# All five queues in written order, weight transfers gated on landed inputs, and four input buffers in a fused linear-attention and mixture kernel

## The chip, the cores and the metric

The kernel runs on one core of a Trainium2 chip. The metric is device time in microseconds (us) of one execution; lower is better. A profile of one execution shows the engines PE (TensorE matmuls), PEld (TensorE weight loads), DVE (VectorE), ACT (ScalarE), POOL (GpSimd) and SP (SyncE, which here only issues transfers).

## The reference

Two layers follow each other. The first is a linear attention with a decaying state; for each batch `b` (4) and head `h` (8), over 768 steps of width 48:

```python
for t in range(S):
    cur = np.einsum('bhd,bhe->bhde', u[None] * kt, vt)
    y[:, :, t] = np.einsum('bhd,bhde->bhe', rt, state + cur)
    state = w[None, :, :, None] * state + np.einsum('bhd,bhe->bhde', kt, vt)
```

Its output, as 3072 rows of 384, is `x` of the second layer, in which each of 4 experts is weighted per row:

```python
p = domain_probs / (domain_probs.sum(-1, keepdims=True) + 1e-09)
for e in range(E):
    h = np.maximum(x @ w1[e], 0.0)          # 384 -> 1024
    out += p[:, e:e + 1] * (h @ w2[e])      # 1024 -> 384
```

## The kernel before

Time is cut into 24 chunks of 128 rows: chunk `ci` is batch `ci % 4` and stretch `ci // 4`. A **super-chunk** `sc` is the four chunks of one stretch, so there are 6. All inputs come as float32; the weights are cast to bfloat16 by their transfer.

**A chunk's attention** goes through these steps, in this order. `pre` (L164) scales r and k by powers of w into the bfloat16 tile RK (L167, L168, DVE), forms `ruk` = r·k·u (L173, L174, POOL), casts v to Vb (L176, POOL), sums ruk into dcoef (L175, DVE) and makes dv (L177, POOL). `stRK` transposes RK on PE (L185, 8 matmuls) and ACT copies the result out (L189). `stAt` multiplies (L196) and DVE applies the mask (L202). `stY` forms the chunk's output on PE (L213, L220); DVE adds dv into Ysb (L224). `stS` updates the state: PE L235, then DVE L244 in the first super-chunk, later DVE L246 and POOL L247. `stX` transposes Ysb (L253) and DVE copies it to xTe (L254), the input of the experts. RK's transpose and stX share one PSUM buffer (tag "tr"); Y, St and the small constants share another (tag "ys").

**The experts.** `l1(e, sc, fb, ...)` is 3 matmuls (L266) and a Relu on ACT (L270); eight values of `fb` make one expert's hidden layer. `l2(e, sc, s)` is 8 matmuls of 384 columns for one chunk (L279), scaled and accumulated on DVE (L285, L287). One pair (e, sc) for a whole super-chunk is a **slot**: 8 l1 of 512 columns, in groups of two, and after each group one l2 of the slot before. Expert 0 of the first super-chunk is not a slot: it is done chunk by chunk (`fill`, L322), l1 with 128 columns. There follow 23 slots; numbered from 0, slots 0 to 2 are experts 1 to 3 of super-chunk 0, slot 3 is expert 0 of super-chunk 1. A counter `carry` inserts attention steps of later chunks between the groups: 10/12 of a step per group in slots 0 and 1, then 5/12 (L365).

**What sets the order.** PE's and POOL's queues are in written order (L318). DVE, ACT and SP are not: a scheduler puts their instructions in an order of its own. `pre` runs up to two chunks ahead of stRK (LEAD, L350). SP issues the loads of r, k and v (L80, three per chunk, six buffers each) and the stores (L290). POOL issues the eight weight transfers: w1 of expert 0 as its first instruction (L85), w2 of expert 0 after `pre(0)`, and the rest after `pre` of chunks 2 to 7 (table `after`, L296). `late_consts` (L132) prepares the decay wC and the normalised expert weights p_nat: p is normalised as 24 x 512, then transposed by PE (L151).

## Time and profile before

| what | value |
|---|---|
| three runs | 348.68, 345.33, 348.07 us; median 348.07 us |
| the profiled execution | 350.93 us, of which the span from first to last instruction is 348.9 us |
| busy in the span | PE 299.3 us (86%), DVE 171.0, ACT 143.3, POOL 108.0 us |
| transfers | 25.96 MB; loads and stores of SP 19.32 MB, weights of POOL 6.29 MB |
| mean granted TensorE clock | 0.964 of full speed |

Busy time counts an engine's instructions; the ends of matmuls are modelled, so busy time of PE is not the same as PE at full speed. "Granted clock" is the share of 2.4 GHz that the chip allowed TensorE in a stretch; the two levels are 1.2 and 2.4 GHz, so 0.76 is a mixture of both. The profiled execution is one of its own; it took 0.8% longer than the median of the three runs.

### The profile page before, as it was taken

The page shows a single profiled execution, that of the slowest core. Times are in us where ns is not written, and L with a number is a line of the kernel's source. Part 1 is how long each engine was busy: PE and PEld are TensorE (multiplying, and loading weights), DVE is VectorE, ACT ScalarE, POOL GpSimd, SP SyncE. Part 2 cuts the span into 40 slices and gives each one's busy share as a digit, 9 for nine tenths or more (in the row PEclk, how much of TensorE's full clock was granted, in tenths as well). Part 3 has the DMA queues.
Part 4 walks back from the last instruction along what each step waited for, and adds up shares of the span by engine and source line. Part 5 has one row for each costly group of instructions (what it writes and reads, how often), then busy time and mean ns, then how long its engine had stood idle before and what let it go on. Part 6 is the DMA issues. An engine that isn't in the chain of part 4 may idle for free.

```text
span 348.9 us, 5568 instructions
## 1 busy us (share of the span) xinstructions
PE 299.3 (86%) x2193; PEld 172.7 (50%) x2229; DVE 171.0 (49%) x333; ACT 143.3 (41%) x245; POOL 108.0 (31%) x145
## 2 busy tenths in 40 slices
PE   0026477767799999999999999999899999999995
PEld 0025455434455555555555555555455555555553
DVE  3498475555655556465546545553534243222223
...
GB/s 131 209 177 189 182 198 207 175 185 143 70 68 49 111 70 69 21 48 121 91 17 68 2 0 92 1 4 0 2 45 47 0 2 0 27 65 0 2 0 90
DMA packets 84457, 25.96 MB, mean 74 GB/s; under 512 B 75448, under 2 KB 82872, under 8 KB 84432
## 3 DMA queue, kind: packets, MB, share of 16 engines
q1 hardware_dynamic: 78672, 19.32, 25.8%
q0 software_dynamic: 5760, 6.29, 11.0%
...
q14 instruction: 8, 0.07, 0.1%
...
## 4 chain that ended last, share of the span: by engine, by line
PE 74%; POOL 11%; DVE 6%; issue 5%; SPq 3%; DMA 1%; POOLq 0%; DVEq 0%
PE out_ps L279 34%; PE hT_ps L266 32%; PE RKT_ps L185 3%; POOL ruk L174 3%; POOL ruk L173 3%; SPq L80 2%; PE At_ps L196 2%; POOL dv L177 1%; POOL S L247 1%; PE Y_ps L220 1%; DVE AtM L202 1%; PE Y_ps L213 1%; POOL Vb L176 1%; PE St_ps L235 1%; SPq L88 1%
## 5 line engine op out<-in xcount | busy, mean ns | idle before, releaser
L270 ACT ACTIVATE hTs<-hT_ps 128x512 bf16<-128x512 f32 (+1 forms) x216 | 116.6, 551 | 146.8 <-PE hT_ps L266 144.0
L266 PE MATMUL hT_ps<-xTe,w_sb 128*128 128x512 bf16 (+1 forms) x612 | 145.6, 366 | 3.3 <-DVE xTe L254 1.4
L279 PE MATMUL out_ps<-w_sb,hTs 128*128 128x384 bf16 x768 | 141.1, 328 | 0.0
L279 PEld LDWEIGHTS <-hTs 128*128 128x128 bf16 x768 | 73.5, 98 | 50.9 <-issue 1.0
L266 PEld LDWEIGHTS <-w_sb 128*128 128x128 bf16 x648 | 59.1, 103 | 50.6 <-issue 3.5
L287 DVE SCALAR_TENSOR_TENSOR oacc<-out_ps,p_nat,oacc 128x384 f32<-128x384 f32 x72 | 44.4, 616 | 73.0 <-PE out_ps L279 72.7
L247 POOL TENSOR_TENSOR S<-Tn,wC 64x192 bf16<-64x192 f32 x32 | 19.4, 605 | 111.5 <-DVE Tn L246 110.3
L189 ACT COPY RKT<-RKT_ps 128x1024 bf16<-128x1024 bf16 x24 | 24.3, 1012 | 45.6 <-PE RKT_ps L185 45.6
L185 PE MATMUL RKT_ps<-ident,RK 128*128 128x128 bf16 x192 | 16.8, 237 | 28.5 <-DVE xTe L254 14.3
L175 DVE TENSOR_REDUCE dcoef<-ruk 128x8 f32<-128x384 f32 x24 | 13.2, 551 | 48.9 <-POOL ruk L174 48.9
L185 PEld LDWEIGHTS <-RK 128*128 128x128 bf16 x192 | 14.2, 106 | 35.5 <-issue 18.3
L202 DVE TENSOR_TENSOR AtM<-At_ps,mask 128x512 bf16<-128x512 f32 x48 | 30.7, 681 | 0.1
L173 POOL TENSOR_TENSOR ruk<-Rt,Kt 128x384 f32<-128x384 f32 x24 | 24.4, 1015 | 9.4 <-DMA Kt<-in_k_dram 8.0
L285 DVE TENSOR_SCALAR oacc<-out_ps,p_nat 128x384 f32<-128x384 f32 x24 | 14.8, 616 | 23.5 <-PE out_ps L279 23.4
L174 POOL TENSOR_TENSOR ruk<-ruk,U_sd 128x384 f32<-128x384 f32 x24 | 24.9, 1039 | 2.2 <-DMA U_sd<-in_u_dram 0.4
L177 POOL TENSOR_TENSOR dv<-Vt,dcoef 128x384 f32<-128x384 f32 x24 | 20.2, 840 | 16.4 <-DVE dcoef L175 13.9
L167 DVE TENSOR_TENSOR RK<-Rt,W_sd 128x384 bf16<-128x384 f32 x24 | 16.1, 673 | 14.5 <-DMA Rt<-in_r_dram 6.1
L224 DVE TENSOR_TENSOR Ysb<-Y_ps,dv 128x384 bf16<-128x384 f32 x24 | 13.4, 557 | 11.0 <-PE Y_ps L220 11.0
L168 DVE TENSOR_TENSOR RK<-Kt,W_sd 128x384 bf16<-128x384 f32 x24 | 15.4, 643 | 0.6
L220 PE MATMUL Y_ps<-Vb,AtM 128*128 128x48 bf16 x192 | 9.8, 188 | 5.7 <-DVE AtM L202 5.7
L176 POOL CAST Vb<-Vt 128x384 bf16<-128x384 f32 x24 | 12.8, 532 | 0.0
L246 DVE TENSOR_TENSOR Tn<-S,St_ps 64x192 f32<-64x192 bf16 x32 | 11.1, 347 | 1.5 <-PE St_ps L235 1.0
...
## 6 DMA issues: line engine op xcount, KB each, us to landing
...
Rt<-in_r_dram SPq DMA_DIRECT2D x24, 192.0 KB, 4.4
Kt<-in_k_dram SPq DMA_DIRECT2D x24, 192.0 KB, 3.6
Vt<-in_v_dram SPq DMA_DIRECT2D x24, 192.0 KB, 3.7
out_dram<-oacc SPq DMA_DIRECT2D x24, 192.0 KB, 1.8
logw_bc<-in_w_dram SPq DMA_DIRECT2D x1, 192.0 KB
U_sd<-in_u_dram SPq DMA_DIRECT2D x1, 192.0 KB, 7.7
...
```

What stands on the lines that cost most here:

```text
L173: nc.gpsimd.tensor_mul(ruk, Rt, Kt)
L174: nc.gpsimd.tensor_mul(ruk, ruk, U_sd)
L176: nc.gpsimd.tensor_copy(Vb, Vt)
L177: nc.gpsimd.tensor_mul(dv, Vt, dcoef.to_broadcast((128, H, D)))
L185: nc.tensor.transpose(ps[:, i, q, :], s["RK"][:, i, 2 * q:2 * q + 2, :].rearrange("p a b -> p (a b)"), ident)
L189: nc.scalar.copy(s["RKT"], ps)
L202: nc.vector.tensor_mul(s["AtM"][:, j], ps[:, j], mask[:, None, :].to_broadcast((128, NP, C)))
L247: nc.gpsimd.tensor_mul(S_new[pr, :, cl], Tn[pr], wCb)
L266: nc.tensor.matmul(ps[:, 0:n, :].rearrange("p a b -> p (a b)"), w1_sb[:, e, db, fb * 128:(fb + 1) * 128], xTe[:, db, s0:s0 + n, :].rearran ...
L270: nc.scalar.activation(hTs[:, fb, s0:s0 + n, :], ps[:, 0:n, :], AF.Relu)
L279: nc.tensor.matmul(ps, hTs[:, fb, s, :], w2_sb[:, e, fb, :], start=(fb == 0), stop=(fb == NFB - 1))
L287: nc.vector.scalar_tensor_tensor(oaccs[ci], in0=ps, scalar=pe, in1=oaccs[ci], op0=ALU.mult, op1=ALU.add)
```

## The change

- All five queues, DVE, ACT and SP among them, are put in written order.
- `pre` is split. `pre_a` has the RK products, ruk and Vb; `pre_b` has the reduction, dv and the issue of one later chunk's load. Neither runs ahead by LEAD any longer; each chunk has six steps instead of five, and its steps are not interleaved with those of the chunk before, but for chunks 2 and 3.
- Input buffers go from six to four. The loads of chunks 0 to 2 are issued first, each later one in `pre_b` of the chunk three before it.
- Each weight transfer is preceded on POOL by a copy of one element of that chunk's r into the weight tile (table `gated`), so that it can't start before this r has landed. w1 of expert 0 waits for r of chunk 0, w2 of expert 0 for chunk 1, expert 1 for chunk 3, expert 2 for chunk 4, expert 3 for chunk 6.
- The raw p is transposed, and normalised after that as 128 x 24 (`p_consts`), behind the first chunk's attention. The state tiles are cleared at the start.
- Two l1 of slot 0 are done ahead, before the last chunk of super-chunk 0 is finished. Slots 0 to 2 take 0.72 of a step per group, and later ones 0.5.

```diff
-    NIN = 6
+    NIN = 4
     NRK = 4
-    LEAD = 2
...
-    logw_bc = consts.tile([128, HD], F32)
-    nc.sync.dma_start(logw_bc, w.rearrange("h d -> (h d)")[None, :].to_broadcast((128, HD)))
-    load_w1(0)
+    w_bc = consts.tile([128, HD], F32)
+    nc.sync.dma_start(w_bc, w.rearrange("h d -> (h d)")[None, :].to_broadcast((128, HD)))
     load(0)
+
+    wrow = consts.tile([NP, 2, P2], F32)
+    nc.vector.memset(wrow, 1.0)
+    nc.sync.dma_start(wrow[:, :, 0:D], w.rearrange("(q j) d -> q j d", j=2))
     U_sd = consts.tile([128, H, D], F32)
     nc.sync.dma_start(U_sd.rearrange("p h d -> p (h d)"),
                       u.rearrange("h d -> (h d)")[None, :].to_broadcast((128, HD)))
-    load(1)
-
-    wrow = consts.tile([NP, 2, P2], F32)
-    nc.vector.memset(wrow, 1.0)
-    nc.sync.dma_start(wrow[:, :, 0:D], w.rearrange("(q j) d -> q j d", j=2))
     prow = consts.tile([TOTC, C, E], F32)
     nc.sync.dma_start(prow, moe_domain_probs.rearrange("(n p) e -> n p e", p=C))
+    load(1)
+    load(2)
...
+    RKB = [consts.tile([128, 2, H, P2], BF16, name=f"RK{i}") for i in range(NRK)]
+    for t in RKB:
+        nc.vector.memset(t[:, :, :, D:P2], 0.0)
+
+    Sbd = [[consts.tile([128, NP, 2 * D], BF16, name=f"S{b}_{i}") for i in range(2)]
+           for b in range(B)]
+    for b in range(B):
+        for i in range(2):
+            nc.vector.memset(Sbd[b][i], 0.0)
...
-    def late_consts():
-        for b in range(B):
-            for i in range(2):
-                nc.vector.memset(Sbd[b][i], 0.0)
+    def w_consts():
         ps = psum.tile([128, NP], F32, tag="ys", bufs=1, name="w_ps")
         nc.tensor.transpose(ps, wrow.rearrange("q j d -> q (j d)"), ident_f[0:NP, 0:NP])
         nc.vector.tensor_copy(wC, ps)
         for _ in range(7):
             nc.vector.tensor_mul(wC, wC, wC)
-        p_sum = consts.tile([TOTC, C, 1], F32)
-        nc.vector.reduce_sum(p_sum, prow, axis=AX.X)
-        nc.vector.tensor_scalar(p_sum, p_sum, scalar1=1e-9, scalar2=None, op0=ALU.add)
-        p_rec = consts.tile([TOTC, C, 1], F32)
-        nc.vector.reciprocal(p_rec, p_sum)
-        p_e = consts.tile([TOTC, E, C], F32)
-        nc.vector.tensor_mul(p_e, prow.rearrange("n p e -> n e p"),
-                             p_rec.rearrange("n p o -> n o p").to_broadcast((TOTC, E, C)))
+
+    def p_consts():
         pp = psum.tile([128, E, TOTC], F32, tag="ys", bufs=1, name="p_ps")
         for e in range(E):
-            nc.tensor.transpose(pp[:, e, :], p_e[:, e, :], ident_f[0:TOTC, 0:TOTC])
-        nc.vector.tensor_copy(p_nat, pp)
+            nc.tensor.transpose(pp[:, e, :], prow[:, :, e], ident_f[0:TOTC, 0:TOTC])
+        p_sum = consts.tile([128, TOTC, 1], F32)
+        nc.vector.reduce_sum(p_sum, pp.rearrange("p e n -> p n e"), axis=AX.X)
+        nc.vector.tensor_scalar(p_sum, p_sum, scalar1=1e-9, scalar2=None, op0=ALU.add)
+        p_rec = consts.tile([128, TOTC, 1], F32)
+        nc.vector.reciprocal(p_rec, p_sum)
+        nc.vector.tensor_mul(p_nat, pp,
+                             p_rec.rearrange("p n o -> p o n").to_broadcast((128, E, TOTC)))
...
-
-    def pre(ci):
+    loaded = [3]
+
+    def pre_a(ci):
         Rt, Kt, Vt = ins.pop(ci)
+        if ci in gated:
+
+            for load_w, t in gated[ci]:
+                nc.gpsimd.tensor_copy(t, Rt[0:1, 0, 0:1])
+                load_w()
         RK = RKB[ci % NRK]
         nc.vector.tensor_mul(RK[:, 0, :, 0:D], Rt, W1_sd)
         nc.vector.tensor_mul(RK[:, 1, :, 0:D], Kt, W2_sd)
         ruk = work.tile([128, H, D], F32, tag="ruk", name="ruk")
-        dcoef = work.tile([128, H, 1], F32, tag="dcoef", name="dcoef")
         Vb = work.tile([128, H, D], BF16, tag="Vb", name="Vb")
-        dv = work.tile([128, H, D], F32, tag="dv", name="dv")
         nc.gpsimd.tensor_mul(ruk, Rt, Kt)
         nc.gpsimd.tensor_mul(ruk, ruk, U_sd)
-        nc.vector.reduce_sum(dcoef, ruk, axis=AX.X)
         nc.gpsimd.tensor_copy(Vb, Vt)
-        nc.gpsimd.tensor_mul(dv, Vt, dcoef.to_broadcast((128, H, D)))
-        st[ci] = dict(RK=RK, Vb=Vb, dv=dv)
+        st[ci] = dict(RK=RK, Vb=Vb, ruk=ruk, Vt=Vt)
+
+    def pre_b(ci):
+        s = st[ci]
+        dcoef = work.tile([128, H, 1], F32, tag="dcoef", name="dcoef")
+        dv = s["dv"] = work.tile([128, H, D], F32, tag="dv", name="dv")
+        nc.vector.reduce_sum(dcoef, s["ruk"], axis=AX.X)
+        nc.gpsimd.tensor_mul(dv, s["Vt"], dcoef.to_broadcast((128, H, D)))
+        if loaded[0] < TOTC:
+            load(loaded[0])
+            loaded[0] += 1
...
-    state = {"loaded": 2, "pre": 0}
-
-    after = {0: [lambda: load_w2(0)], 2: [lambda: load_w1(1)], 3: [lambda: load_w2(1)],
-             4: [lambda: load_w1(2)], 5: [lambda: load_w2(2)],
-             6: [lambda: load_w1(3)], 7: [lambda: load_w2(3)]}
-
-    def load_next():
-        if state["loaded"] < TOTC:
-            load(state["loaded"])
-            state["loaded"] += 1
-
-    def pre_upto(n):
-        while state["pre"] < min(n, TOTC):
-            pre(state["pre"])
-            for f in after.get(state["pre"], []):
-                f()
-            state["pre"] += 1
-            load_next()
...
-    with tc.manual_schedule(engines={ET.PE, ET.Pool}):
...
-        for ci in range(SUB):
-            pre_upto(ci + 1)
-            stRK(ci)
-            if ci == 0:
-                late_consts()
-            run(prev)
-            stAt(ci)
-            run(prev)
-            stY(ci)
-            run(prev)
-            stS(ci)
-            stX(ci)
-            prev = fill(ci)
...
+    def gate(f, sb, e):
+        return (lambda: f(e)), sb[0:1, e, 0, 0:1]
+
+    gated = {0: [gate(load_w1, w1_sb, 0)],
+             1: [gate(load_w2, w2_sb, 0)],
+             3: [gate(load_w1, w1_sb, 1), gate(load_w2, w2_sb, 1)],
+             4: [gate(load_w1, w1_sb, 2), gate(load_w2, w2_sb, 2)],
+             6: [gate(load_w1, w1_sb, 3), gate(load_w2, w2_sb, 3)]}
+
+    def l1s(e, sc, s0, n, fbs=range(NFB)):
+        for fb in fbs:
+            l1(e, sc, fb, s0, n)
+
+    with tc.manual_schedule(engines={ET.PE, ET.Pool, ET.DVE, ET.Activation, ET.SP}):
+
+        pre_a(0)
+        stRK(0)
+        pre_b(0)
+        stAt(0)
+        w_consts()
+        stY(0)
+        stS(0)
+        stX(0)
+        p_consts()
+        pre_a(1)
+        l1s(0, 0, 0, 1)
+        stRK(1)
+        pre_b(1)
+        stAt(1)
+        stY(1)
+        stS(1)
+        stX(1)
+        l2(0, 0, 0)
+        l1s(0, 0, 1, 1)
+        pre_a(2)
+        l2(0, 0, 1)
+        stRK(2)
+        pre_b(2)
+        stAt(2)
+        pre_a(3)
+        stY(2)
+        stS(2)
+        stRK(3)
+        stX(2)
+        pre_b(3)
+        l1s(0, 0, 2, 1)
+        stAt(3)
+        l2(0, 0, 2)
+        stY(3)
+        stS(3)
+        l1s(1, 0, 0, 3, (0, 1))
+        stX(3)
+        l1s(0, 0, 3, 1)
+        l1s(1, 0, 3, 1, (0, 1))
...
-            for ci in range(first, last + 1):
-                new, old = ci < last, ci > first
-                if new:
-                    yield lambda ci=ci: (pre_upto(ci + LEAD), stRK(ci))
-                if old:
-                    yield lambda ci=ci: stY(ci - 1)
-                    yield lambda ci=ci: stS(ci - 1)
-                if new:
-                    yield lambda ci=ci: stAt(ci)
-                if old:
-                    yield lambda ci=ci: stX(ci - 1)
+            for ci in range(first, last):
+                yield lambda ci=ci: pre_a(ci)
+                yield lambda ci=ci: (stRK(ci), pre_b(ci))
+                yield lambda ci=ci: stAt(ci)
+                yield lambda ci=ci: stY(ci)
+                yield lambda ci=ci: stS(ci)
+                yield lambda ci=ci: stX(ci)
...
         steps = att_steps(SUB, TOTC)
-        carry = 0.0
         l2s = [lambda: l2(0, 0, SUB - 1)]
-        pre_upto(SUB + 1)
+        carry = -1.0
         for si, (e, sc) in enumerate(slots):
-            per = (10 if si < 2 else 5) / 12
+            if si == E - 1:
+                carry = 0.5
+            per = 0.72 if si < E - 1 else 0.5
             for q in range(4):
                 for g in range(3):
-                    if g < 2:
+                    if g == 2:
+                        if l2s:
+                            l2s.pop(0)()
+                    elif si > 0 or q > 0:
                         l1(e, sc, 2 * q + g, 0, SUB)
-                    elif l2s:
-                        l2s.pop(0)()
                     carry += per
                     while carry >= 1:
                         carry -= 1
-                        run(steps)
+                        f = next(steps, None)
+                        if f:
+                            f()
```

Three places show the order of the queues; names carry a buffer number (`Rt_74` is chunk 0's r, `W1_sd` and `W2_sd` are the powers of w).

POOL at the start of the program, before (from the first weight transfer to the second):

```order
L68 DMA w1_sb_70<-in_moe_w1_dram 128x3x1024
L100 ISA
L100 IOTA iota_i_94 128x1
masks.py:197 MEMSET ident_96 128x128
masks.py:65 MEMSET mask_101 128x128
masks.py:199 AFFINE_SELECT ident_96<-ident_96 128x128
masks.py:66 AFFINE_SELECT mask_101<-mask_101 128x128
L173 TENSOR_TENSOR ruk_151<-Rt_75,Kt_76 128x384
L174 TENSOR_TENSOR ruk_151<-ruk_151,U_sd_81 128x384
L176 CAST Vb_153<-Vt_77 128x384
L177 TENSOR_TENSOR dv_154<-Vt_77,dcoef_152 128x384
L71 DMA w2_sb_71<-in_moe_w2_dram 128x8x384
```

and in the changed program, from the end of the mask on (L168 is the one-element copy):

```order
masks.py:66 AFFINE_SELECT mask_106<-mask_106 128x128
L168 CAST w1_sb_70<-Rt_74 1x1
L67 DMA w1_sb_70<-in_moe_w1_dram 128x3x1024
L175 TENSOR_TENSOR ruk_154<-Rt_74,Kt_75 128x384
L176 TENSOR_TENSOR ruk_154<-ruk_154,U_sd_83 128x384
L177 CAST Vb_155<-Vt_76 128x384
L185 TENSOR_TENSOR dv_171<-Vt_76,dcoef_170 128x384
L168 CAST w2_sb_71<-Rt_87 1x1
L70 DMA w2_sb_71<-in_moe_w2_dram 128x8x384
```

The first weight transfer moved from ahead of everything to behind the landing of chunk 0's r; the second from behind dv of chunk 0 to behind the landing of chunk 1's r.

DVE during chunk 0's attention, before:

```order
L140 TENSOR_TENSOR wC_133<-wC_133 128x4
L167 TENSOR_TENSOR RK2_119<-Rt_137,W1_sd_113 128x8x48
L140 TENSOR_TENSOR wC_133<-wC_133 128x4
L147 TENSOR_TENSOR p_e_201<-prow_92,p_rec_199 24x512
L140 TENSOR_TENSOR wC_133<-wC_133 128x4
L175 TENSOR_REDUCE dcoef_249<-ruk_248 128x8
L140 TENSOR_TENSOR wC_133<-wC_133 128x4
L152 COPY p_nat_134<-p_ps_203 128x96
L140 TENSOR_TENSOR wC_133<-wC_133 128x4
L202 TENSOR_TENSOR AtM_218<-At_ps_209,mask_101 128x512 x2
L168 TENSOR_TENSOR RK2_119<-Kt_138,W2_sd_115 128x8x48
L224 TENSOR_TENSOR Ysb_230<-Y_ps_221,dv_154 128x384
```

and in the changed program, from chunk 0's second RK product on:

```order
L172 TENSOR_TENSOR RK0_113<-Kt_75,W2_sd_142 128x8x48
L184 TENSOR_REDUCE dcoef_170<-ruk_154 128x8
L212 TENSOR_TENSOR AtM_189<-At_ps_180,mask_106 128x512 x2
L136 COPY wC_146<-w_ps_192 128x4
L138 TENSOR_TENSOR wC_146<-wC_146 128x4 x7
L234 TENSOR_TENSOR Ysb_211<-Y_ps_202,dv_171 128x384
L254 TENSOR_TENSOR S0_1_122<-St_ps_213,wC_146 64x4x48 x2
L264 COPY xTe_225<-xT_ps_221 128x3x128
L145 TENSOR_REDUCE p_sum_232<-p_ps_227 128x24
L146 TENSOR_SCALAR p_sum_232<-p_sum_232 128x24
L148 RECIPROCAL p_rec_235<-p_sum_232 128x24
L149 TENSOR_TENSOR p_nat_147<-p_ps_227,p_rec_235 128x96
```

The normalisation of p went from ahead of the mask product (AtM) to behind xTe; the powers of wC went from ahead of AtM to between AtM and Ysb; the RK products of chunk 2, which stood among them, are no longer there.

POOL in slot 1, where w1 of expert 3 is issued, before and after (S0, S1: state of batches 0 and 1):

```order
L177 TENSOR_TENSOR dv_725<-Vt_376,dcoef_723 128x384
L68 DMA w1_sb_70<-in_moe_w1_dram 128x3x1024
L247 TENSOR_TENSOR S0_0_125<-Tn_774,wC_133 64x4x48 x2
L173 TENSOR_TENSOR ruk_814<-Rt_490,Kt_491 128x384
L174 TENSOR_TENSOR ruk_814<-ruk_814,U_sd_81 128x384
```

```order
L185 TENSOR_TENSOR dv_792<-Vt_431,dcoef_791 128x384
L257 TENSOR_TENSOR S1_0_123<-Tn_858,wC_146 64x4x48 x2
L168 CAST w1_sb_70<-Rt_497 1x1
L67 DMA w1_sb_70<-in_moe_w1_dram 128x3x1024
L168 CAST w2_sb_71<-Rt_497 1x1
L70 DMA w2_sb_71<-in_moe_w2_dram 128x8x384
L175 TENSOR_TENSOR ruk_894<-Rt_497,Kt_498 128x384
```

The transfer that stood ahead of the state update of chunk 4 now stands behind that of chunk 5, and both transfers of the expert stand ahead of chunk 6's ruk.

## Rows read from the trace of the kernel before

**Rows 1.** Windows: stretch, busy us (count) of PE, PEld, DVE, ACT, POOL, clock, DMA share, GB/s.
```profile
0.00:27.30 27.30, 4.06 (x36) 2.81 (x37) 16.31 (x45) 5.22 (x6) 14.07 (x24) 1.00 0.96 173
27.30:62.50 35.20, 24.74 (x236) 18.44 (x237) 21.41 (x36) 11.70 (x38) 18.12 (x21) 0.76 1.13 195
62.50:94.90 32.40, 23.46 (x209) 13.73 (x213) 18.10 (x36) 12.02 (x18) 14.32 (x19) 0.89 0.80 145
94.90:288.20 193.30, 190.30 (x1410) 107.43 (x1436) 99.70 (x193) 90.49 (x143) 61.49 (x82) 1.00 0.17 42
```

**Rows 2.** Timeline of chunk 0: start, us, engine, line, tile, idle before and releaser.
```profile
1.25 0.93 POOL L68 DMA_DIRECT2D w_sb<-in_moe_w_dram  x1 [0.81 <-POOLq L393]
7.28 0.60 ACT L118 ACTIVATE W_sd<-logw_bc,e_neg 128x384 f32<-128x384 f32 x1
11.23 0.99 POOL L173 TENSOR_TENSOR ruk<-Rt,Kt 128x384 f32<-128x384 f32 x1 [8.04 <-DMA Kt<-in_k_dram]
12.67 0.99 POOL L174 TENSOR_TENSOR ruk<-ruk,U_sd 128x384 f32<-128x384 f32 x1 [0.45 <-DMA U_sd<-in_u_dram]
15.42 1.01 ACT L189 COPY RKT<-RKT_ps 128x1024 bf16<-128x1024 bf16 x1 [7.54 <-PE RKT_ps L185]
21.28 0.62 PE L151 MATMUL p_ps<-ident_f,p_e 24*128 24x24 f32 x4 [5.70 <-DVE p_e L147]
21.83 0.61 PE L196 MATMUL At_ps<-RKT 64*128 64x128 bf16 x8
22.60 1.27 DVE L202 TENSOR_TENSOR AtM<-At_ps,mask 128x512 bf16<-128x512 f32 x2
26.89 0.36 DVE L254 COPY xTe<-xT_ps 128x384 bf16<-128x384 bf16 x1
```

**Rows 3.** Weight tiles, then loads of r (median): us from issue to landing.
```profile
DMA to landing us min/median/max: 8.0/9.2/10.2
Rt<-in_r_dram SPq DMA_DIRECT2D x24, 192.0 KB, 4.4
```

**Rows 4.** Timeline of PE: the same pieces of work at either clock.
```profile
27.31 1.01 PE L185 MATMUL RKT_ps<-ident,RK 128*128 128x128 bf16 x8 [0.89 <-DVE xTe L254]
28.11 1.49 PE L266 MATMUL hT_ps<-xTe,w_sb 128*128 128x128 bf16 x12
30.07 0.89 PE L266 MATMUL hT_ps<-xTe,w_sb 128*128 128x128 bf16 x12
45.40 2.73 PE L279 MATMUL out_ps<-w_sb,hTs 128*128 128x384 bf16 x8
60.65 0.61 PE L185 MATMUL RKT_ps<-ident,RK 128*128 128x128 bf16 x8
61.09 1.46 PE L279 MATMUL out_ps<-w_sb,hTs 128*128 128x384 bf16 x8
```

**Rows 5.** Timeline: ruk beside an RK product; then L167's ns (min/median/max).
```profile
28.80 1.20 POOL L174 TENSOR_TENSOR ruk<-ruk,U_sd 128x384 f32<-128x384 f32 x1
29.07 1.35 DVE L168 TENSOR_TENSOR RK<-Kt,W_sd 128x384 bf16<-128x384 f32 x1
L167 DVE TENSOR_TENSOR RK<-Rt,W_sd x24: 533/559/1867, 7.4 to 222.8; 128x384 bf16<-128x384 f32 x24
```

**Rows 6.** Timeline of PE, and one state update on POOL, from slot 0 on.
```profile
72.29 1.01 PE L185 MATMUL RKT_ps<-ident,RK 128*128 128x128 bf16 x8 [3.58 <-DVE xTe L254]
76.15 2.37 PE L266 MATMUL hT_ps<-xTe,w_sb 128*128 128x512 bf16 x5
94.94 1.24 PE L266 MATMUL hT_ps<-xTe,w_sb 128*128 128x512 bf16 x5
95.70 1.29 POOL L247 TENSOR_TENSOR S<-Tn,wC 64x192 bf16<-64x192 f32 x2 [3.85 <-DVE Tn L246]
248.13 0.61 PE L185 MATMUL RKT_ps<-ident,RK 128*128 128x128 bf16 x8 [1.59 <-DVE xTe L254]
338.56 6.66 PE L279 MATMUL out_ps<-w_sb,hTs 128*128 128x384 bf16 x40
```

More of the change, by code (lines that the diff above doesn't have):

```diff
@@ L112 @@
                             op0=ALU.mult, op1=ALU.add)
-    nc.scalar.activation(logw_bc, logw_bc, AF.Ln)
     W1_sd = consts.tile([128, H, D], F32)
-    nc.scalar.activation(W1_sd.rearrange("p h d -> p (h d)"), logw_bc, AF.Exp,
-                         scale=e_pos[:, 0:1])
     W2_sd = consts.tile([128, H, D], F32)
-    nc.scalar.activation(W2_sd.rearrange("p h d -> p (h d)"), logw_bc, AF.Exp,
-                         scale=e_neg[:, 0:1])
-    RKB = [consts.tile([128, 2, H, P2], BF16, name=f"RK{i}") for i in range(NRK)]
-    for t in RKB:
-        nc.vector.memset(t[:, :, :, D:P2], 0.0)
-    Sbd = [[consts.tile([128, NP, 2 * D], BF16, name=f"S{b}_{i}") for i in range(2)]
-           for b in range(B)]
+    nc.scalar.activation(w_bc, w_bc, AF.Ln)
+    for W_sd, ex in ((W1_sd, e_pos), (W2_sd, e_neg)):
+        nc.scalar.activation(W_sd.rearrange("p h d -> p (h d)"), w_bc, AF.Exp,
+                             scale=ex[:, 0:1])
     wC = consts.tile([128, NP], F32)
     p_nat = consts.tile([128, E, TOTC], F32)
-    def late_consts():
-        for b in range(B):
-            for i in range(2):
-                nc.vector.memset(Sbd[b][i], 0.0)
+    def w_consts():
         ps = psum.tile([128, NP], F32, tag="ys", bufs=1, name="w_ps")
@@ L313, in run @@
-    def run(gen):
-        f = next(gen, None)
-        if f:
-            f()
-    with tc.manual_schedule(engines={ET.PE, ET.Pool}):
-        load_next()
-        load_next()
-        def fill(ci):
-            for half in range(2):
-                yield lambda half=half: [l1(0, 0, fb, ci, 1) for fb in range(4 * half, 4 * half + 4)]
-            yield lambda: l2(0, 0, ci)
-        prev = iter(())
-        for ci in range(SUB):
-            pre_upto(ci + 1)
-            stRK(ci)
-            if ci == 0:
-                late_consts()
-            run(prev)
-            stAt(ci)
-            run(prev)
-            stY(ci)
-            run(prev)
-            stS(ci)
-            stX(ci)
-            prev = fill(ci)
-        run(prev)
-        run(prev)
-        def att_steps(first, last):
-            for ci in range(first, last + 1):
-                new, old = ci < last, ci > first
-                if new:
-                    yield lambda ci=ci: (pre_upto(ci + LEAD), stRK(ci))
-                if old:
-                    yield lambda ci=ci: stY(ci - 1)
-                    yield lambda ci=ci: stS(ci - 1)
-                if new:
-                    yield lambda ci=ci: stAt(ci)
-                if old:
-                    yield lambda ci=ci: stX(ci - 1)
```

## The prediction

> **What bounds the kernel now.** I read the windows first, cut where the program changes character: chunk 0's attention (to 27.3 us), the rest of super-chunk 0 with expert 0 chunk by chunk (to 62.5), slots 0 and 1 (to 94.9), slots 2 to 17. From 94.9 on PE is busy 190.3 of 193.3 us at full clock [rows 1]: nothing that reorders the other queues can win much there. Ahead of it PE does 4.1 of 27.3, 24.7 of 35.2 and 23.5 of 32.4 us, at clocks of 1.00, 0.76 and 0.89 [rows 1], so 42.7 us of the first 94.9 are idle and part of the rest runs at half speed. The DMA share there is 0.96, 1.13 and 0.80 [rows 1]. So the second thing to read is who ends the waits at the start: in the timeline of chunk 0, PE and POOL wait for k (to 11.2 us), for u (to 12.7) and for the normalised p (to 21.3), while the first weight transfer has been in the queues since 1.25 us [rows 2].
>
> **The change, part by part.** Times are from the start of the span; the profiled execution took 350.93 us for a span of 348.9, so 2.0 us lie around it, and it is 2.86 us above the median of the three runs.
>
> *A, to chunk 0's xTe.* Before: 26.89 + 0.36 = 27.25 us [rows 2]. Now k and u no longer share the queues with w1 of expert 0, which waits for r, and p is normalised later. What can't move is the power of w, ready at 7.28 + 0.60 = 7.88 [rows 2]. From there: RK's second product 0.56 [rows 5], the second half of its transposes 0.5 (half of 1.01 [rows 4]), ACT's copy 1.01 [rows 2], which gives 10.0; then the stretch from At to xTe as before, 27.25 − 21.83 = 5.4 [rows 2]. In that stretch another chunk's RK product stood ahead of Ysb on DVE; the powers of wC now take its place, so I change nothing: xTe at 15.5. Lower bound: this, since ACT's result comes from w's own load. Upper bound: k and u land as late as before (11.2 and 12.7); u then gives ruk at 13.7, and with the cast, the sum and dv behind it Ysb comes 3 us later, xTe at 18.7. I take 15.5, since all that stood ahead of those loads is gone. POOL now has the weight's issue, 0.93 us [rows 2], ahead of ruk; it fits in, as r lands about 4.4 us [rows 3] after its issue and k later. Gain **11.8 us** (8.5 to 11.8).
>
> w1 of expert 0 is needed for the first l1, behind 0.6 us of p's transposes: 16.1. If r lands at about 5.6 and the transfer takes 8.0 to 10.2 from issue [rows 3], it is there between 13.8 and 16: free, but without room. w2 likewise: r of chunk 1 at about 14 or 15, landing 22 to 25, needed at about 24.5.
>
> *B, to the end of expert 0's l2 for chunk 3.* Before: from 27.25 to 61.09 + 1.46 = 62.55 [rows 4], 35.3 us. The new program is a plain chain. With the quick and the slow values of the same pieces [rows 4]: p's transposes 0.6; four chunks' l1, 24 short matmuls each, 4 x 1.8 to 3.0; four l2, 1.3 to 2.7, of which one covers most of a mask product; attention of chunks 1 and 2, transposes 0.6 to 1.0, copy 1.0 and At to xTe 4.7 (the 5.4 without the foreign product, my estimate): 2 x 6.3 to 6.7; chunk 3's transposes and copy, which stX of chunk 2 waits for in the shared buffer, 1.6 to 2.0; chunk 3 from At on, 4.7; the two early l1 of expert 1, in all 1.3 to 2.6. Sum, quick: 0.6 + 7.2 + 3.9 + 12.6 + 1.6 + 4.7 + 1.3 = 32; slow: 0.6 + 12 + 9.5 + 13.4 + 2 + 4.7 + 2.6 = 45. In this stretch the clock was 0.76 [rows 1], about half way between the two levels: I take 38. It ends at 53.5: B gives back **2.7 us** (from a gain of 3 to a loss of 10). That this chain is no shorter than before is no error: before, the work of several chunks overlapped, but waited for data.
>
> *C, slots 0 to 2.* Before, slots 0 and 1 with the attention of four chunks took 94.9 − 62.5 = 32.4 [rows 1], and slot 2 about 12.0 (193.3 less the 1.6 of D, over 16 slots), of which one chunk's attention, which the new order has done by then, is 1.5 (below): 42.9 for the same work. Now the four chunks are spread over three slots. Pure PE work: an l1 is 3 x 0.216 = 0.65 (5 in 1.24 with the tail of the last [rows 6]), an l2 6.66 / 5 = 1.33 [rows 6], a chunk 12.0 − 8 x 0.65 − 4 x 1.33 = 1.5; 22 l1, 8 l2 and 4 chunks are 31. Waits on top: chunk 4 stands in slot 0, where there are no l2 to put between its steps; its At comes straight behind its transposes and waits 1.1 for ACT's copy, Y follows one l1 after At and waits 0.7 for the mask product, and RK 0.5: 2.3. For chunks 5 to 7 I put 0.8 each: 2.4. Expert 3: its w1 is now issued behind chunk 5's state update on POOL, and S alone takes 1.29 us [rows 6], with Tn ahead of it and the copy behind about 2; with 8.0 to 10.2 to landing it comes 10 to 12 after St, and PE reaches the first l1 of slot 2 after three l2, four l1 and a chunk's rest, about 8.5: a wait of 1.5 to 3.6. Without the contention of the first 80 us it should be at the low end: 1.5. A part of the slots at half speed, as after the wait of 3.58 (five matmuls in 2.37 for 1.24 [rows 6]): 0.8. Together 38, between 35 and 43: gain **4.9 us** (0 to 8).
>
> *D, slots 3 on.* The one wait of 1.59 us late in the kernel [rows 6], where the last `pre` runs ahead, should go, as no chunk runs ahead any more: gain **1.6 us**. Otherwise the steps lie two groups apart, and the mask product, 1.27 [rows 2], has an l2 and an l1 beside it. Four input buffers cost nothing: a load still goes out about three chunks, over 30 us, ahead of use. Stores on SP wait only for what PE has just finished.
>
> Sum: 11.8 − 2.7 + 4.9 + 1.6 = 15.6; 350.93 − 15.6 = 335.3, and from the median 348.07 − 15.6 = 332.5, say **333 us**. The profiled execution is the slow one of the four, so I count from the median.
>
> **The rivals.**
>
> *Weights late (15%).* Each gate moves a transfer later, and PE comes to them earlier. For it: two of the five landings above have no room. Against: a landing of 8 to 10 us was measured in full queues. Price: 3.6 at slot 2 in place of 1.5, as much again at expert 0, and half speed behind each (1.1 per five matmuls): 8 more, 341.
>
> *All at the quick clock (8%).* B 32 and C 36: 8 less, 325.
>
> *The start isn't freed (7%).* The change does nothing to the bytes: share 0.96 and more while they last [rows 1]. If the loads of chunks 0 to 3 are limited by the queues and not by the weights ahead of them, A ends at 18.7 and B near its slow end, 45: 333 + 3.2 + 7 = 343, and with a late weight 346 to 351: no change.
>
> *Slower: RK and ruk collide (7%).* An RK product that ran beside ruk took 1.35 us, and the longest 1.87, instead of 0.56 [rows 5]: for a pair 2.1 more. Before, the scheduler set most of them elsewhere, as the median of 0.559 shows. Written order puts both behind the same landed chunk, in `pre_a`. In the steady slots, by the order of the steps, ruk can start about 2.3 us after St (once S is done) and RK 3.5 after it, with about 0.8 of room before RK's transposes. A collision that costs up to 0.8 is therefore hidden; the full 2.1 would cost 1.3 in each of 20 chunks, 26 us: 359. It turns slower from 1.6 on. Against it: half of ruk is done when RK begins.
> The Trainium skill, "SBUF — State Buffer", section "Who interferes with whom", has it that a VectorE instruction with two SBUF inputs and a GpSimd instruction that reads SBUF exclude each other for the whole instruction. The trace agrees (1.35 beside 1.20 [rows 5]); by that rule alone RK would wait for a whole ruk each time, which is this rival.
>
> **How the numbers follow.** The forecast, 333, has 63%, with a range of its own of 328 to 339. Within 1% is 344.6 to 351.6, about what a measurement can tell from no change here. Faster: forecast, late weights and quick clock, 0.86; same 0.07; slower 0.07. The range 325 to 342 holds the forecast, two thirds of the late weights and half of the quick clock, near 0.77, with the bounds of B and C inside.
>
> **What would show it.** Right: xTe of chunk 0 near 15.5; first weight issue near 6; l2 of chunk 3 ending near 53.5; slot 3 starting near 92 (before, slot 2 started at 94.9); a wait for a weight at slot 2 of 1 to 2 us. Wrong: POOL still waiting for k beyond 9 us (A), PE waiting for RK in every slot from 3 on, with RK products above 1 us (collision), or a gap of over 3 us at the first l1 of slots 0 to 2 (weights).

## The result, and the profile after

The changed kernel takes **330.72 us** (median of four runs, 330.01 to 333.24) against 348.38 for the kernel before beside it (345.33 to 348.82): ratio **0.953**, 95% interval 0.946 to 0.959. The forecast was 333, range 325 to 342. The profiled execution took 333.24 us, span 331.4, so like the one of before it is above its median, by 2.5 us (2.9 there); differences between two profiles are therefore not the differences of the medians.

The windows of the changed kernel, cut at the four points that the prediction named; the columns are those of [rows 1]:
```profile
0.00:15.90 15.90, 3.46 (x35) 2.47 (x35) 8.88 (x33) 5.22 (x6) 5.68 (x16) 1.00 0.81 151
15.90:51.80 35.90, 25.85 (x237) 18.98 (x237) 17.63 (x35) 12.49 (x39) 17.88 (x24) 0.90 1.07 182
51.80:89.90 38.10, 32.51 (x265) 18.08 (x269) 24.08 (x44) 16.77 (x26) 18.38 (x26) 1.00 0.69 115
89.90:283.20 193.30, 191.93 (x1429) 109.03 (x1453) 116.41 (x201) 90.37 (x146) 68.61 (x88) 1.00 0.26 57
```
Chunk 0 is shorter by 11.35 us (15.90 for 27.25), the stretch to the end of expert 0's l2 of chunk 3 is as long as before (35.9 for 35.3), slots 0 to 2 take 38.1, and behind them PE is busy 99% of the time, where [rows 1] had 98%.

The timeline of chunk 0 (start, us, engine, line, tile, idle before and releaser), which answers to [rows 2]:
```profile
5.24 0.18 POOL L168 CAST w_sb<-Rt 1x1 bf16<-1x1 f32 x1 [3.50 <-DMA Rt<-in_r_dram]
5.73 0.94 POOL L67 DMA_DIRECT2D w_sb<-in_moe_w_dram  x1 [0.31 <-POOL w_sb L168]
6.69 1.01 POOL L175 TENSOR_TENSOR ruk<-Rt,Kt 128x384 f32<-128x384 f32 x1
9.29 1.01 ACT L199 COPY RKT<-RKT_ps 128x1024 bf16<-128x1024 bf16 x1 [1.87 <-PE RKT_ps L195]
9.47 0.99 POOL L176 TENSOR_TENSOR ruk<-ruk,U_sd 128x384 f32<-128x384 f32 x1 [1.77 <-DMA U_sd<-in_u_dram]
15.54 0.36 DVE L264 COPY xTe<-xT_ps 128x384 bf16<-128x384 bf16 x1
```
POOL no longer waits for k (8.04 us in [rows 2]): the first weight goes out at 5.73, behind r.

PE's pieces, which answer to [rows 4] and [rows 6]:
```profile
16.19 2.74 PE L276 MATMUL hT_ps<-xTe,w_sb 128*128 128x128 bf16 x24
25.89 2.72 PE L289 MATMUL out_ps<-w_sb,hTs 128*128 128x384 bf16 x8
50.33 1.46 PE L289 MATMUL out_ps<-w_sb,hTs 128*128 128x384 bf16 x8
76.45 1.24 PE L276 MATMUL hT_ps<-xTe,w_sb 128*128 128x512 bf16 x5 [0.73 <-DMA w_sb<-in_moe_w_dram]
```
The first l1 follows xTe at once. Three of four blocks of 24 short matmuls took 2.7 us, near the long value. One weight is late, at slot 2, by 0.73 us.

A collision of an RK product with ruk, which answers to [rows 5]:
```profile
59.72 1.19 POOL L175 TENSOR_TENSOR ruk<-Rt,Kt 128x384 f32<-128x384 f32 x1
59.98 1.35 DVE L172 TENSOR_TENSOR RK<-Kt,W_sd 128x384 bf16<-128x384 f32 x1
61.38 0.40 PE L195 MATMUL RKT_ps<-ident,RK 128*128 128x128 bf16 x4 [0.87 <-DVE RK L172]
```
It costs 0.87 us at this one place; behind it PE waits for no RK product again.

The waits that the stage table hides are in the list of who waited for whom (us in total, times, longest). PE's waits for DVE in the kernel before:
```profile
PE RKT_ps L185 <- DVE xTe L254: 14.3, 7, 3.6
PE RKT_ps L185 <- DVE RK L167: 8.0, 1, 8.0
PE RKT_ps L185 <- DVE RK L168: 6.1, 1, 6.1
PE Y_ps L220 <- DVE AtM L202: 5.7, 7, 2.2
```
and in the changed one:
```profile
PE RKT_ps L195 <- DVE RK L171: 8.8, 2, 8.2
PE St_ps L245 <- DVE Ysb L234: 4.2, 4, 1.3
PE Y_ps L230 <- DVE AtM L212: 3.5, 8, 0.8
```
The largest wait before, 14.3 us in seven waits for the copy xTe, is gone (0.9 us is left, ahead of l1). It can't come from chunk 0 alone (there it is 0.89, [rows 4]). The experiments start from this.

### The profile page after: what moved, and what is told of

The parts are those of the page before. It is cut to its first block, busy times and chain, and to the rows that moved or that the text cites. A ratio compares the mean times of both kernels' runs of the same rounds, so it can differ in the third digit from the quotient of the medians.

```text
span 331.4 us, 5583 instructions
## 1 busy us (share of the span) xinstructions
PE 298.0 (90%) x2200; PEld 172.2 (52%) x2235; DVE 179.3 (54%) x332; ACT 142.7 (43%) x247; POOL 110.6 (33%) x153
## 3 DMA queue, kind: packets, MB, share of 16 engines
q0 software_dynamic: 5760, 6.29, 11.8%
## 4 chain that ended last, share of the span: by engine, by line
PE 82%; DVE 7%; DMA 3%; issue 2%; ACT 2%; SPq 1%; POOL 1%; ACTq 0%; DVEq 0%; POOLq 0%
PE out_ps L289 37%; PE hT_ps L276 34%; PE RKT_ps L195 3%; PE At_ps L206 2%; DMA w_sb<-in_moe_w_dram 2%; DVE AtM L212 2%; ACT RKT L199 2%; PE St_ps L245 1%; DVE RK L172 1%; PE xT_ps L263 1%; PE Y_ps L230 1%; DMA U_sd<-in_u_dram 1%; DVE Ysb L234 1%; DVE RK L171 1%; SPq L79 1%
## 5 line engine op out<-in xcount | busy, mean ns | idle before, releaser
L280 ACT ACTIVATE hTs<-hT_ps 128x512 bf16<-128x512 f32 (+2 forms) x218 | 116.2, 547 | 144.3 <-PE hT_ps L276 139.1
L276 PE MATMUL hT_ps<-xTe,w_sb 128*128 128x512 bf16 (+1 forms) x619 | 143.7, 363 | 3.4 <-DVE xTe L264 0.9
L276 PEld LDWEIGHTS <-w_sb 128*128 128x128 bf16 x654 | 60.1, 103 | 47.7 <-issue 1.5
L257 POOL TENSOR_TENSOR S<-Tn,wC 64x192 bf16<-64x192 f32 x32 | 16.0, 501 | 81.1 <-DVE Tn L256 79.9
L176 POOL TENSOR_TENSOR ruk<-ruk,U_sd 128x384 f32<-128x384 f32 x24 | 24.7, 1030 | 3.6 <-DMA U_sd<-in_u_dram 1.8
L171 DVE TENSOR_TENSOR RK<-Rt,W_sd 128x384 bf16<-128x384 f32 x24 | 21.6, 900 | 3.4 <-ACT W_sd L127 3.4
L195 PEld LDWEIGHTS <-RK 128*128 128x128 bf16 x192 | 12.8, 101 | 14.4 <-DVE RK L171 9.8
L172 DVE TENSOR_TENSOR RK<-Kt,W_sd 128x384 bf16<-128x384 f32 x24 | 19.5, 813 | 0.0
L177 POOL CAST Vb<-Vt 128x384 bf16<-128x384 f32 x24 | 17.0, 709 | 0.0
L206 PE MATMUL At_ps<-RKT 64*128 64x128 bf16 x192 | 10.2, 229 | 5.5 <-ACT RKT L199 5.5
```

Source lines behind the costliest of these rows:

```text
L171: nc.vector.tensor_mul(RK[:, 0, :, 0:D], Rt, W1_sd)
L172: nc.vector.tensor_mul(RK[:, 1, :, 0:D], Kt, W2_sd)
L176: nc.gpsimd.tensor_mul(ruk, ruk, U_sd)
L195: nc.tensor.transpose(ps[:, i, q, :], s["RK"][:, i, 2 * q:2 * q + 2, :].rearrange("p a b -> p (a b)"), ident)
L276: nc.tensor.matmul(ps[:, 0:n, :].rearrange("p a b -> p (a b)"), w1_sb[:, e, db, fb * 128:(fb + 1) * 128], xTe[:, db, s0:s0 + n, :].rearran ...
L280: nc.scalar.activation(hTs[:, fb, s0:s0 + n, :], ps[:, 0:n, :], AF.Relu)
```

## The experiments

**1. One part undone.** First the gates, then the late p, each undone in the changed kernel.

Without gates (e1):
```diff
-                nc.gpsimd.tensor_copy(t, Rt[0:1, 0, 0:1])
```
Expected: 

> The changed kernel without the eight one-element copies; every weight transfer stays where it is in POOL's queue. Theory (the start was freed by holding back w1 of expert 0): that transfer is issued near 1.7 us again, k and u land near 11 to 12.7, and xTe of chunk 0 ends near 18.9 instead of 15.9; the other gates cost and win little: 334 us. Rival 1 (the gates do nothing, order alone made the gain): 331. Rival 2 (all gates matter, loads and weights collide in many places): 338 or more.

The old p_consts, normalised as 24 x 512, ahead of At of chunk 0, and wC with it (e3):
```diff
...
         pre_b(0)
-        stAt(0)
         w_consts()
+        p_consts()
+        stAt(0)
...
```
Expected: 

> The changed kernel with p normalised as before (24 x 512, then transposed), and this, with wC, ahead of chunk 0's At. Theory (p's chain ended last at the start): DVE waits in order for p's own load and then works about 4 us on p; xTe of chunk 0 near 21 instead of 15.9, of which about 2 come back because chunk 1 no longer has p's work on DVE: 334 to 335. Rival (p was hidden behind k and u anyway): 331.

Measured: 333.46 us (ratio 0.954, 0.948 to 0.960) and 335.65 (0.960, 0.955 to 0.965). The first xTe ended at 20.3 and 21.2, so each loses 4.4 to 5.3 us of the 11.35 at chunk 0. In e1 k is not late (ruk begins at 6.15), only u is, and that is about half of the loss: the mask product begins at 13.30 for 11.01, behind the sum that waits for u; most of the rest is wC's seven small products, 3.47 us for 1.34, beside POOL's ruk. Expert 0's l2 of chunk 3 ended at 54.2 and 54.5, against 51.8 in the changed kernel. By the medians e1 costs 2.7 us, as expected, and e3 4.9, a little more than expected, but both intervals overlap with that of the changed kernel. Neither undoes the gain: over 12 us of it stay.

**2. The two parts alone** (e6), the kernel before with the gate on expert 0's w1 and the late p, scheduler as it was.
```diff
-    load_w1(0)
...
+        if ci == 0:
+            nc.gpsimd.tensor_copy(w1_sb[0:1, 0, 0, 0:1], Rt[0:1, 0, 0:1])
+            load_w1(0)
...
             stX(ci)
+            if ci == 0:
+                p_consts()
```
Expected: 

> The kernel before with two parts of the change: w1 of expert 0 gated on chunk 0's r, and p transposed first and normalised behind chunk 0's attention. All else as before, the scheduler's order for DVE too, which now puts chunk 1's first RK product ahead of chunk 0's second. If gate and p alone free the start (the forecast's term A as written): 348.4 - 11 = 337. If written order is needed with them, because chunk 1's r lands behind the gated weights near 15: xTe of chunk 0 near 22 to 24, and 344 to 347.

Measured: **348.26** (0.995, 0.991 to 0.999): nearly nothing. Without the order these two free the start only in part. DVE's timeline in it:
```profile
9.87 0.63 DVE L169 TENSOR_TENSOR RK<-Rt,W_sd 128x384 bf16<-128x384 f32 x1 [1.84 <-DMA Rt<-in_r_dram]
15.15 0.16 DVE L137 COPY wC<-w_ps 128x4 f32<-128x4 f32 x1 [3.71 <-PE w_ps L136]
22.69 0.36 DVE L256 COPY xTe<-xT_ps 128x384 bf16<-128x384 bf16 x1
```
At 9.87 chunk 1's product stands ahead of chunk 0's second product and waits for chunk 1's r; xTe comes at 23.05 instead of 15.90 (27.25 before). By the two profiles e6 is 6.6 us ahead at the end of chunk 3's l2 (55.95 for 62.55) and gives 2.3 of them back in slots 0 and 1 (slot 2 starts at 90.62 for 94.94); PE's waits for xTe ahead of the transposes are 12.7 us in six waits, close to the 14.3 of before. The spans of the profiles differ by 4.1 us, the medians by only 0.6; where the rest goes is not shown.

**3. Which queue.** The changed kernel with some queues left to the scheduler: DVE, ACT and SP (e4), DVE alone (e7), SP alone (e8).
```diff
-    with tc.manual_schedule(engines={ET.PE, ET.Pool, ET.DVE, ET.Activation, ET.SP}):
+    with tc.manual_schedule(engines={ET.PE, ET.Pool, ET.Activation, ET.SP}):   # e7
```
Expected of e4: 

> The changed kernel, with DVE, ACT and SP left to the scheduler; PE and POOL as they are. The scheduler's DVE order has chunk 1's two RK products ahead of chunk 0's sum and mask product. Theory: chunk 1's r now lands near 15.5 us, so in that order chunk 0 waits for it, xTe of chunk 0 near 21 to 22 and the total near 336. Rival (gates and p make the gain, the order of these queues adds nothing): 331.

Expected of e7: 

> The changed kernel with VectorE alone left to the scheduler; ScalarE, SyncE, GpSimd and TensorE stay in written order. Theory (the price of an order that is not written lies in VectorE's queue: products of a later chunk stand ahead of the current chunk's work and wait for a late r): 352 to 362 us, with waits of 5 us or more for r at the first product of a chunk, and the first xTe at 20 to 22 us. Rival (SyncE's queue: the loads themselves start later when the scheduler places them): 330 to 336 us, and the loss is found where SyncE is left to it.

Expected of e8: 

> The changed kernel with SyncE alone left to the scheduler. Theory (VectorE's queue): 330 to 334 us, no wait for r over 2 us behind the first chunk. Rival (SyncE's queue): 345 to 362 us.

Measured: e4 **362.23** (1.038, 1.032 to 1.043), where both theories had missed the size; e7 **358.68** (1.034, 1.027 to 1.040); e8 330.30 (0.951, 0.946 to 0.955), like the changed kernel. So it is DVE's queue; ACT's was not left to the scheduler by itself, but the intervals of e4 and e7 overlap. Two rows of e4's timeline of DVE and the row of PE that follows:
```profile
53.13 0.56 DVE L171 TENSOR_TENSOR RK<-Rt,W_sd 128x384 bf16<-128x384 f32 x1 [5.79 <-DMA Rt<-in_r_dram]
53.72 0.36 DVE L264 COPY xTe<-xT_ps 128x384 bf16<-128x384 bf16 x1
54.13 2.72 PE L276 MATMUL hT_ps<-xTe,w_sb 128*128 128x128 bf16 x24 [6.58 <-DVE xTe L264]
```
DVE stands 5.79 us before a product of a later chunk whose r has not landed; the copy xTe, ready to go, stands behind it, and PE waits 6.58. In e4 DVE waited for r eight times, 21.1 us in all; in e7 ten times, 30.2. That this is worse than the kernel before, with its own scheduled order, may come from the gates, the four buffers or the new sequence; these were not separated.

**4. The order alone.** The kernel before with all queues in written order (e9), and with DVE's alone (e12); nothing else changed.
```diff
-    with tc.manual_schedule(engines={ET.PE, ET.Pool}):
+    with tc.manual_schedule(engines={ET.PE, ET.Pool, ET.DVE}):   # e12
```
Expected of e9: 

> The kernel before with all five queues in written order and nothing else changed: no gates, p ahead as it was, six buffers, its own sequence of steps. Theory (the order frees the start only together with the gate on the first weight and the late p): 343 to 347 us, the first xTe at 22 to 26 us, since r still lands behind w1's packets and p's nine small instructions still stand ahead. Rival 1 (the written order is the whole gain): 333 to 337 us. Rival 2 (its dcoef, now at the head of VectorE's queue, waits for GpSimd's product): 350 us or more.

Expected of e12: 

> The kernel before with VectorE in written order besides TensorE and GpSimd, and nothing else changed; ScalarE and SyncE stay with the scheduler. Theory (the 10.6 us of the written order are VectorE's): 337 to 340 us, and no RK product of a later chunk ahead of the current chunk's work. Rival (ScalarE's or SyncE's order carries it): 344 to 348 us.

Measured: **337.97** (0.972, 0.968 to 0.976) and **338.28** (0.965, 0.961 to 0.969). My theory for e9 had missed: the order alone brings 10.6 us of the changed kernel's 17.7, and it is DVE's. Yet chunk 0 has hardly gained (xTe ends at 26.5 and 26.3). The windows of e12, cut at its own xTe of chunk 0, its l2 of chunk 3 and its slot 2:
```profile
0.00:26.20 26.20, 4.12 (x36) 2.69 (x36) 13.43 (x38) 5.22 (x6) 9.05 (x18) 1.00 0.97 175
26.20:54.70 28.50, 20.62 (x238) 15.17 (x241) 17.90 (x36) 11.38 (x38) 14.41 (x18) 1.00 1.09 189
54.70:83.20 28.50, 22.99 (x209) 13.07 (x212) 20.68 (x39) 11.92 (x18) 22.07 (x28) 0.94 1.14 199
```
The middle stretch takes 28.5 us for 35.3, slots 0 and 1 take 28.5 for 32.4 [rows 1]. In the middle stretch PE's busy time for the same work falls from 24.7 to 20.6 us, with a granted clock of 1.00 for 0.76, and its idle time from 10.5 to 7.9: more than half of the gain there is shorter pieces, the rest fewer waits. (The two profiles differ by 14.4 us in all, the medians by 11.3.) The reason for the waits stands in DVE's timeline of the kernel before, in rows that the prediction did not read; rows between are left out:
```profile
35.62 0.95 DVE L167 TENSOR_TENSOR RK<-Rt,W_sd 128x384 bf16<-128x384 f32 x1 [1.83 <-DMA Rt<-in_r_dram]
37.77 0.36 DVE L254 COPY xTe<-xT_ps 128x384 bf16<-128x384 bf16 x1
42.96 0.56 DVE L167 TENSOR_TENSOR RK<-Rt,W_sd 128x384 bf16<-128x384 f32 x1 [4.24 <-DMA Rt<-in_r_dram]
43.43 0.55 DVE L175 TENSOR_REDUCE dcoef<-ruk 128x8 f32<-128x384 f32 x1
43.90 1.28 DVE L202 TENSOR_TENSOR AtM<-At_ps,mask 128x512 bf16<-128x512 f32 x2
70.10 0.55 DVE L175 TENSOR_REDUCE dcoef<-ruk 128x8 f32<-128x384 f32 x1 [2.55 <-POOL ruk L174]
71.89 0.35 DVE L254 COPY xTe<-xT_ps 128x384 bf16<-128x384 bf16 x1
```
At 35.62 DVE had stood 1.83 us for the r of a later chunk; the copy xTe, whose transposes were done at 34.8, stood behind it, and PE waited 3.35 us for it. Then the same with a mask product: At had been ready since 41; the mask product stood behind a later chunk's RK, and PE waited 2.23 us for it. At 70.10 it is not a late load: the sum of a later chunk had waited 2.55 us for POOL's ruk, and the copy behind it ended PE's longest wait, 3.58 us [rows 6]. In e12 the products follow the copy xTe without a wait:
```profile
34.31 0.36 DVE L254 COPY xTe<-xT_ps 128x384 bf16<-128x384 bf16 x1
34.70 0.56 DVE L167 TENSOR_TENSOR RK<-Rt,W_sd 128x384 bf16<-128x384 f32 x1
```
and of PE's 14.3 us of waits for xTe 0.3 are left:
```profile
PE RKT_ps L185 <- DVE xTe L254: 0.3, 2, 0.2
```
A little comes back elsewhere: PE's waits for RK's products grow from 14.1 to 15.7 us, those for Ysb from 2.7 to 4.9.

**5. Order, gate and late p, with the old sequence of steps** (e10): e6 with the line of experiment 4, for all five queues.
```diff
-    with tc.manual_schedule(engines={ET.PE, ET.Pool}):
+    with tc.manual_schedule(engines={ET.PE, ET.Pool, ET.DVE, ET.Activation, ET.SP}):
```
Expected: 

> The kernel before with the gate on expert 0's first weight, p normalised late in its transposed form, and all five queues in written order; its own sequence of steps on TensorE, six buffers. Theory (these three together are the freed start, worth some 11 us, and the new sequence of steps adds the rest): 335 to 339 us, first xTe at 16 to 18 us. Rival (the new sequence of steps behind the start is what counts): 343 to 348 us, with the first xTe at 16 to 18 us and the gain lost behind it.

Measured: **333.59** (0.960, 0.956 to 0.964), 1.4 below the theory; xTe of chunk 0 at 21.1, not 16 to 18, since PE waited until 15.35 for wrow, with At behind it in its queue; only the changed kernel loads wrow earlier. So gate and late p are worth 4.4 us once the order is written, and all the rest of the change (the load order, the new sequence, four buffers) 2.9 by the medians, with overlapping intervals. The middle stretch is 30.5 us here, as in e9 (29.6). In the changed kernel it is 35.9, and 32.9 in e8, whose start is the same: the early start is partly given back there, because in the new sequence little lies beside the attention of chunks 1 to 3 (the next experiment tests this).

**6. The old interleaving on the new start** (e11).
```diff
+        for ci in range(1, SUB):
+            l1s(0, 0, ci - 1, 1, range(0, 4))
+            stAt(ci)
+            l1s(0, 0, ci - 1, 1, range(4, 8))
+            stY(ci)
...
```
Expected: 

> The changed kernel with another sequence of steps for chunks 1 to 3 alone: the first layer of expert 0 for chunk c is put between the transposes, At and Y of chunk c+1, the RK product of the next chunk stands between Y and xTe, p's normalisation stands behind chunk 1's transposes; start, gates, load order, slots as in the changed kernel. Theory (what the changed kernel wins at chunk 0 it gives back in part, since its chunks 1 to 3 are a chain with nothing beside it, some 33 to 36 us from xTe of chunk 0 to the end of expert 0's second layer for chunk 3, against 30 in the two kernels that keep the old interleaving): xTe of chunk 0 at 15 to 16, the end of that layer at 43 to 47, 325 to 328 us. Rival 1 (that stretch is set by the landing of the chunks' r, k and v behind the weights, not by the sequence): DVE waits for Rt or Kt there, 330 to 334 us. Rival 2 (the stretch gets shorter, and PE then waits for the weights of experts 1 and 2 instead): waits of over 2 us for w_sb, 328 to 331 us.

Measured: **327.64** (0.937, 0.933 to 0.941), below the interval of the changed kernel. Its windows:
```profile
0.00:15.90 15.90, 3.18 (x32) 2.15 (x32) 9.10 (x34) 5.22 (x6) 7.58 (x18) 1.00 0.85 164
15.90:44.00 28.10, 20.39 (x237) 15.64 (x238) 19.02 (x34) 11.02 (x39) 17.17 (x23) 1.00 1.12 189
```
The middle stretch is 28.1 us, 7.8 less than in the changed kernel's profile and 4.8 less than in e8's. Of the 7.8, 5.5 are PE's busy time (20.4 us for 25.9, for the same work) and 2.3 its idle time, so here too the larger part is shorter pieces. The wait at slot 2 stayed at 0.71. Left is a collision, which here lies on the path:
```profile
30.20 1.81 DVE L171 TENSOR_TENSOR RK<-Rt,W_sd 128x384 bf16<-128x384 f32 x1
30.58 1.01 POOL L175 TENSOR_TENSOR ruk<-Rt,Kt 128x384 f32<-128x384 f32 x1
31.67 1.20 POOL L176 TENSOR_TENSOR ruk<-ruk,U_sd 128x384 f32<-128x384 f32 x1
31.93 1.34 DVE L172 TENSOR_TENSOR RK<-Kt,W_sd 128x384 bf16<-128x384 f32 x1
34.12 0.61 PE L195 MATMUL RKT_ps<-ident,RK 128*128 128x128 bf16 x8 [2.86 <-DVE xTe L264]
```

**7. Four more moves** (e15) on e11. `keep_x` is stX that keeps the chunk's tiles for stS; `l2` calls it between its matmuls and its scaling.
```diff
-        w_consts()
         stY(0)
-        stS(0)
-        stX(0)
+        keep_x(0)
         pre_a(1)
         stRK(1)
-        p_consts()
+        w_consts()
+        stS(0)
...
             stAt(ci)
+            if ci == 1:
+                p_consts()
+            elif ci == 2:
+                pre_a(3)
...
-                pre_a(ci + 1)
-                l2(0, 0, ci - 1)
-                s = st[ci]
-                stX(ci)
-                st[ci] = s
+                if ci == 1:
+                    pre_a(2)
+                l2(0, 0, ci - 1, lambda: keep_x(ci))
...
-             6: [gate(load_w1, w1_sb, 3), gate(load_w2, w2_sb, 3)]}
+             5: [gate(load_w1, w1_sb, 3), gate(load_w2, w2_sb, 3)]}
```
Expected: 

> The kernel of the interleaved chunks 1 to 3 with four moves that its trace points to: wC's small multiplications and chunk 0's state behind xTe of chunk 0 (they stood 1.5 us ahead of Ysb); p's normalisation behind At of chunk 1; chunk 3's RK product ahead of Ysb of chunk 2, so that it doesn't run beside GpSimd's ruk (there its two products took 1.81 and 1.34 us), and the scaling of expert 0's result behind xTe instead of ahead of it; expert 3's gate at chunk 5 in place of 6 (a wait of 0.71 us at slot 2). Theory (these DVE instructions stand on the way to xTe and to the next transposes): xTe of chunk 0 at 14.5, the wait of 2.86 us ahead of chunk 3's transposes under 1 us, the end of expert 0's second layer for chunk 3 at 40 to 42 in place of 44, 323 to 326 us. Rival 1 (k of chunks 1 to 3 lands behind the weights, and the chain waits for it instead): the same end at 43 to 44 and 327 to 328 us. Rival 2 (the earlier gate crowds the queues that carry r and k): a new wait for k over 2 us, 328 us or more.

Measured: **324.91** (0.932, 0.927 to 0.936), the best version, though its interval overlaps with e11's. The profile doesn't bear out the theory: xTe of chunk 0 came at 14.25 and the wait of 2.86 fell to 0.28, but the l2 of chunk 3 ended at 44.4 as in e11. The moved constants grew longer in their new place:
```profile
16.90 2.27 DVE L138 TENSOR_TENSOR wC<-wC 128x4 f32<-128x4 f32 x7
22.10 1.01 DVE L146 TENSOR_SCALAR p_sum<-p_sum 128x24 f32<-128x24 f32 x1
```
(1.34 and 0.18 in e11), Y of chunk 1 waits 1.67 us for p_nat, and the l2 behind it took 2.73 us for 1.51 in e11. The wait for expert 3 is gone; expert 1's w1 now has one of 0.51. Why the median is 2.7 lower is not shown: the two profiled executions took 325.62 and 325.73 us.

**8. A busier PE at the start** (e13).
```diff
+        warm(40)      # matmuls ident x ident into an unused PSUM tile
         pre_a(0)
...
```
Expected: 

> The changed kernel with 63 matmuls of 128 columns whose result nobody reads, on TensorE in its waits for chunk 0: 40 ahead of the first transposes, 7 ahead of At, 8 ahead of Y, 8 ahead of the state's product. Theory (the pieces at the low level of the clock, 24 short matmuls in 2.74 and a second layer in 2.72, follow from an idle TensorE in the first 16 us; four or five such pieces cost some 1.3 us each): the first transposes 0.6 us, the first 24 short matmuls 1.6 to 1.9, 325 to 328 us. Rival 1 (the low level comes back in the waits of chunks 1 to 3, whatever went before): quick pieces only to about 20 us, 329 to 331 us. Rival 2 (the extra matmuls push chunk 0's own steps back): xTe of chunk 0 behind 16.5, 331 to 334 us.

Measured: 332.91 (0.950, 0.946 to 0.954), no gain; the theory had missed. Rows of PE in it:
```profile
1.55 3.94 PE L307 MATMUL warm_ps<-ident 128*128 128x128 bf16 x40 [1.55 <-POOL ident masks.py:199]
8.23 1.07 PE L195 MATMUL RKT_ps<-ident,RK 128*128 128x128 bf16 x8 [2.74 <-DVE RK L171]
16.24 2.74 PE L276 MATMUL hT_ps<-xTe,w_sb 128*128 128x128 bf16 x24
24.59 2.76 PE L289 MATMUL out_ps<-w_sb,hTs 128*128 128x384 bf16 x8
```
With PE busy 10.0 of the first 16 us instead of 3.6, its pieces stayed long to about 27 us, and in the changed kernel to about 31; in both, the block of 24 short matmuls near 40 us is long again (2.72 us). What would lift the clock there is open.

## Why the prediction was right, and where not

- **A, 11.8 us: 11.35 measured**, by the steps named. But with gate and late p alone xTe comes at 23.05 (e6), and with DVE's order left to the scheduler in the changed kernel at 22.0 to 22.1 (e4, e7), not at 15.90. That "another chunk's RK product stood ahead of Ysb" was in my text, at no price; the written order of DVE was the condition of more than half of the term. With the order, gate and late p but the old order of loads xTe still comes at 21.1 (e10).
- **B, 38 us: 35.9 measured**, 32.9 in e8. The step that failed as a reading is the sentence that the new chain "is no shorter than before is no error", because the old work "waited for data". In part it waited for DVE: with the same steps and DVE in written order it takes 28.5 to 29.6 (e12, e9), with shorter pieces on PE besides. I had the size of the new chain, but not that the old one with a written DVE queue beats it.
- **C, 38 us: 38.1 measured.** The wait at slot 2 was 0.73 for 1.5.
- **D, 1.6 us:** the wait is gone. From slot 3 on the time was 241.5 (331.4 less 89.9); the terms give 241.8 (a span of 333.3 less 15.5, 38 and 38).
- **The sum is right, its credit is not.** Between the profiles the gain is 17.5 us for 15.6, and the difference is mainly B's. But with chunk 0 ending at 26.5 and 26.3 the order alone still gave 10.6 and 11.3 us (e9, e12), so that A came out does not make it the cause. The terms were differences of stages, and I took the largest of them for the cause.
- **Rivals.** Weights late: 0.73 only, no. Start not freed: no. RK and ruk: the products grew to 900 and 813 ns on average, from 673 and 643 before, but behind chunk 1 PE waited for them 0.87 us in all: the room that I had put at 0.8 held for collisions of this size. In each collided pair shown here the RK product ends 0.40 to 0.42 us behind the end of a ruk, so it did the most of its work only then (alone it takes 0.56). The Trainium skill ("SBUF — State Buffer", "Who interferes with whom") has it that the two exclude each other for the whole instruction; these rows agree. Which of the two goes first they leave open: in e11 the product recorded from 30.20 ends behind a ruk recorded from 30.58. Quick clock (325): not reached by this kernel.
- **Small slips** that change nothing: the idle time of the first 94.9 us is 42.6, not 42.7, and A's steps add up to 15.4, not 15.5.
